# Three first loads on one DMA queue, and a longer run of zero matmuls

## The chip, the cores and the metric

The kernel runs on one core of a Trainium2 chip. A core has TensorE (PE in the profile: matmuls, with PEld for its weight loads), VectorE (DVE), ScalarE (ACT), GpSimd (POOL) and SyncE (SP), which issues DMAs. ACT can issue DMAs too, on a queue of its own; 16 DMA engines serve all queues. The metric is the time of one execution on the device in microseconds (us).

## The reference, cut to what matters

`x` has 2048 rows of 512 columns. One branch is attention with a window of 8 positions at a dilation of 2 and 32 heads of 16; the other is a token mixer over the 2048 rows with a layer norm and a GELU; a sigmoid gate mixes the two.

```python
g = sigmoid((x * gate_w).sum(-1, keepdims=True))
qkv = x @ wqkv                        # 512 x 1536: Wq, Wk, Wv side by side
logits[s, w] = (q[s] . k[s - 2*w]) * 16**-0.5      # w = 0..7, -1e9 before the start
a = (softmax(logits) weighted sum of v[s - 2*w]) @ wo
u = gelu(einsum("sd,sf->df", layernorm(x), w1) + b1)   # f = 1792
b = (u @ w2 + b2).T                   # back to 2048 x 512
out = g * a + (1 - g) * b
```

All tensors are bfloat16. Of the reference only the first product, `x @ wqkv`, matters here, and of it only the part that runs first: rows 0 to 511 of `x` against Wq and Wk.

## The kernel before

**Tiling.** TensorE contracts over the partitions, so it needs x transposed: `XT[p, d, s]` holds column 128·d + p of row s. The 512 columns of x make four slices d = 0..3, the 2048 rows four blocks `sb` of 512. Wq's rows come in the same four slices; the kernel calls each a quarter (128 KB, `ld_w(0, d, 1)` at L447; the first argument 0 is Wq, 1 is Wk, 2 is Wv, the last the number of slices). A group of matmuls for one slice d takes four, one for each output bank.

**Two ways to the transpose.** For block 0, slices 1 to 3 of XT come by a transposing DMA (`ld_xt0`, L470 to L476, issued at L473). Slice 0 comes otherwise: the plain columns 0 to 127 of rows 0 to 511 are loaded as they are into XP (`d_xp`, L479), TensorE transposes them with four matmuls against the identity matrix (`f_tr`, L544: tr0 and tr1), and ACT (L553, `ev_tra`) and VectorE (L555, `ev_trb`) each copy one half of the result into XT. The later blocks of XT come by transposing DMAs of 512 KB (`ld_xt`, L460).

**The zero matmuls.** Before and after the transposes TensorE runs matmuls on constants, whose results nobody reads (`f_warm`, L536, into bank 7): five of 512 columns and one of 256 ahead of the transposes (warm1, warm2), one of 512 behind them (warm3). The change's title calls these columns zeros; the operands are the constant 1.0, and the text keeps the title's word.

**The first projections.** The loop at L633 runs block 0's matmuls (L617): four for Wq with slice 0 (group 1), four each with slices 1, 2 and 3 (groups 2 to 4), then 16 for Wk in two halves. Group 1 waits for the two copies and Wq's first quarter, group 2 for the transposing DMA and Wq's second quarter, and so on; TensorE runs its work in order. ACT copies the finished banks to SBUF (L625 for block 0, L628 after). Then block 1 (32 matmuls), blocks 2 and 3, and Wv follow. Later TensorE works on the attention logits (L696), the mixer's two products (L810, L860) and the output projection (L876); VectorE ends with the sums of L897.

**What sets the order.** `_Sched` collects operations with their reads, writes and an estimated duration, and a list scheduler (L145) sorts each engine's work by estimated start times. For the first loads the estimates of landing are written in by hand (`lands`, L485 to L488), and `chain` (L941) fixes VectorE's and ACT's order for much of the kernel. A DMA belongs to the engine that issues it: `sch.dma("sp", ...)` or `sch.dma("act", ...)`. `after=prev_dma()` keeps SP's first loads in the order in which they are written, and later ones also wait until an earlier load has landed (`throttle`, L433). All direct DMAs are issued from L429.

Before the change SP issues, in this order: the transposing DMA of block 0, Wq's other three quarters, Wk in two halves, rows 0 to 255 of x for the layer norm (L439), the transposing DMA of block 1, and then the rest. ACT issues the plain columns and then Wq's first quarter.

Of the kernel before, what the change touches and what calls it, by code (L numbers as in the profile page):

```python
# [333 lines left out]
def bass_gated_mix__sliding_local_dilated__mixer_token_mlp__prompt_kernel(nc, A_x, A_wqkv, A_wo, B_x, B_w1, B_b1, B_w2, B_b2, gate_w, out, dbg=None):  # L334
    with contextlib.ExitStack() as es:
# [3 lines left out]
        sch = _Sched()  # L339

        x2d = A_x[0]
        xv = x2d.rearrange("(t p) d -> p t d", p=128)
# [72 lines left out]
        A = sch.add  # L415
# [12 lines left out]
        def mk_dma(dst, src):  # L428
            return lambda e: e.dma_start(dst, src)  # L429
# [3 lines left out]
        def throttle():  # L433
            return [init_dmas[-5]] if len(init_dmas) >= 5 else []

        def prev_dma():
            return [init_dmas[-1]] if init_dmas else []

        def ld_x(t0, n, q="sp"):  # L439
            ds = sch.dsem("x%d" % t0)  # L440
            op = sch.dma(q, mk_dma(X[:, t0:t0 + n, :], xv[:, t0:t0 + n, :]), n * 128 * D * 2, ds,
                         writes=["x%d" % t for t in range(t0, t0 + n)], deps=throttle() if q == "sp" else [], after=prev_dma() if q == "sp" else [], name="d_x%d" % t0)
            if q == "sp":
                init_dmas.append(op)
            return op

        def ld_w(tn, d0, n, q="sp"):  # L447
            ds = sch.dsem("wqkv%d_%d" % (tn, d0))
            op = sch.dma(q, mk_dma(WQKV[:, d0:d0 + n, tn * D:(tn + 1) * D], wqkv_v[:, d0:d0 + n, tn * D:(tn + 1) * D]),
                         n * 128 * D * 2, ds, writes=["wqkv%d_%d" % (tn, dt) for dt in range(d0, d0 + n)],  # L450
                         deps=throttle() if q == "sp" and n == 4 else [], after=prev_dma() if q == "sp" else [],
                         issue=0.65 if n == 4 else 0.45, name="d_wp%d_%d" % (tn, d0))
            if q == "sp":
                init_dmas.append(op)
            return op
# [14 lines left out]
        def ld_xt0():  # L470
            ds = sch.dsem("xt0")
            dst = XT[:, 1:4, 0:512]
            op = sch.dma("sp", lambda e: e.dma_start_transpose(dst, x2d[0:512, 128:512]), 512 * 384 * 2, ds, issue=1.25,  # L473
                         writes=XT0[1:4], after=prev_dma(), name="d_xt0")
            init_dmas.append(op)
            return op  # L476

        XP = view("OUTS", BF16, [(128, 4), (1, 128)])
        d_xp = sch.dma("act", mk_dma(XP, xv[:, 0:4, 0:128]), 512 * 128 * 2, sch.dsem("xp"), writes=["outs0"], issue=0.4, name="d_xp")  # L479

        first_loads = [ld_w(0, 0, 1, "act"), ld_xt0(), ld_w(0, 1, 1), ld_w(0, 2, 1), ld_w(0, 3, 1), ld_w(1, 0, 2), ld_w(1, 2, 2),
                       ld_x(0, 2)]
        ld_xt(1)
        first_loads.append(init_dmas[-1])
        for op_, t_ in zip(first_loads, (3.4, 4.6, 5.0, 5.4, 5.8, 6.6, 7.4, 8.2, 10.6)):  # L485
            op_.lands = t_
            op_.deps.clear()
        d_xp.lands = 3.1  # L488
# [11 lines left out]
        def ld_w1(j):  # L500
# [4 lines left out]
            if j < 4:  # L505
# [8 lines left out]
                       writes=["wo"], deps=throttle(), after=prev_dma(), name="d_wo")  # L514
# [4 lines left out]
        for i_, (v_, n_) in enumerate(((B_b1, NFT), (B_b2, NST))):  # L519
            vr = v_.rearrange("(t q j) -> q t j", q=4, j=32)  # L520
            for q_ in range(4):
                sch.dma("sp", mk_dma(psub(BR, 32 * q_, n_, 32 * i_, [(1, 32)]), vr[q_]), n_ * 64, ds_b, reads=["br"],
                        writes=["br_%d_%d" % (i_, q_)], deps=throttle(), after=prev_dma(), name="d_b_%d_%d" % (i_, q_), issue=0.45)
        d_w1.append(ld_w1(3))
        A("dve", lambda e: e.transpose(out=BT, in_=BR), 0.2, reads=["br_%d_%d" % (i_, q_) for i_ in range(2) for q_ in range(4)],
          writes=["btc"], name="t_b")
# [5 lines left out]
        def f_warm(n, w_=D):  # L532
            def fn(e):
                ins = None
                for _ in range(n):
                    ins = e.matmul(ps[:, 7, 0:w_], lhsT=CONE[:, 0:128], rhs=CONE[:, 0:w_], start=True, stop=True)  # L536
                return ins
            return fn

        def f_tr(h):  # L540
            def fn(e):
                ins = None
                for t in range(2):
                    ins = e.matmul(ps[:, 5 + h, 128 * t:128 * t + 128], lhsT=XP[:, 2 * h + t, :], rhs=IDENT, start=True, stop=True)  # L544
                return ins
            return fn
# [2 lines left out]
        w2_ = A("pe", f_warm(1, 256), 0.2, writes=["lg7_0", "lg7_1"], name="warm2", prio=-100)  # L549
        ta_ = A("pe", f_tr(0), 0.215, reads=["outs0", "ident"], writes=["lg5_0", "lg5_1"], after=[w2_], name="tr0", prio=-100)  # L550
        tr_ = A("pe", f_tr(1), 0.215, reads=["outs0", "ident"], writes=["lg6_0", "lg6_1"], after=[ta_], name="tr1", prio=-100)
        w3_ = A("pe", f_warm(1), 0.43, writes=["lg7_0", "lg7_1"], after=[tr_], name="warm3", prio=-100)
        A("act", lambda e: e.activation(out=XT[:, 0, 0:256], in_=ps[:, 5, 0:256], func=AF.Copy), 0.35, reads=["lg5_0", "lg5_1"],  # L553
          writes=["xt0_0"], name="ev_tra", prio=0)
        A("dve", lambda e: e.tensor_copy(out=XT[:, 0, 256:512], in_=ps[:, 6, 0:256]), 0.35, reads=["lg6_0", "lg6_1"],  # L555
          writes=["xt0_0b"], name="ev_trb", prio=0)
# [76 lines left out]
        for (b0, d0, d1, s0, s1) in ((0, 0, 1, 0, 512), (0, 1, 2, 0, 512), (0, 2, 3, 0, 512), (0, 3, 4, 0, 512), (4, 0, 2, 0, 512), (4, 2, 4, 0, 512)):  # L633
            for b in range(b0, b0 + 4):
# [3 lines left out]
                                 writes=fbn[b], after=[last_main[0]], name="pf_%s%d_%d_%d" % (tnames[tn], dl, d0, s0))  # L638
                last_main[0].order.add(w3_)
        for b, (tn, dl) in enumerate(first):  # L640
            A("act", f_evq(tn, dl, 0, b), 0.52, reads=fbn[b] + (["k5pad"] if tn == 1 else []),
              writes=["%s5_%d_0" % (tnames[tn], dl)], name="ev_%s%d_0" % (tnames[tn], dl), prio=0)
# [7 lines left out]
        for (tn, dl, sb) in seq_proj:  # L650
# [4 lines left out]
                             writes=["acc%d" % bank], after=[last_main[0]], name="pj_%s%d_%d" % (tnames[tn], dl, sb), prio=0)  # L655
            A("act", f_evq(tn, dl, sb, bank), 0.62, reads=["acc%d" % bank] + (["k5pad"] if tn == 1 else ["v5pad"] if tn == 2 else []),
              writes=["%s5_%d_%d" % (tnames[tn], dl, sb)], name="ev_%s%d_%d" % (tnames[tn], dl, sb), prio=0)
# [11 lines left out]
                writes=["xa"] + ["wqkv%d_%d" % (tn, dt) for tn in range(3) for dt in range(4)], name="d_xa")  # L669
        for t in range(NST):  # L670
# [5 lines left out]
          writes=["th"], name="g_tanh", prio=0)  # L676
# [31 lines left out]
        for wh in range(2):  # L708
# [6 lines left out]
            for (dl, c0, nc_) in pieces:  # L715
# [5 lines left out]
                  writes=wr, name="qkm_%d_%d_%d" % (wh, dl, c0), prio=0)  # L721
            rd = sum([pbn(b_) for b_ in bufs], []) + PBX[wh] + ["rp"]
            for wl in range(4):
                qop = A("pe", f_qkr(list(enumerate(bufs)), (wl,)), 0.92, reads=rd, writes=["lg%d_0" % (4 + wl), "lg%d_1" % (4 + wl)],
                        name="qkr_%d_%d" % (wh, wl), prio=-100 + wl, delay=BURST_DELAY)
                A("act", (lambda wh_, wl_: (lambda e: e.activation(out=ATT[:, :, 4 * wh_ + wl_, :], in_=ps[:, 4 + wl_, :].rearrange("p (h c) -> p h c", h=2), func=AF.Copy)))(wh, wl),  # L726
                  0.55, reads=["lg%d_0" % (4 + wl), "lg%d_1" % (4 + wl)], writes=["lw%d" % (4 * wh + wl)],
                  name="lev_%d_%d" % (wh, wl), prio=0)
# [60 lines left out]
        for k_, u in enumerate(USEQ):  # L789
# [7 lines left out]
            for (nm, n_, du) in (("ava", 4, 2.25), ("avb", 2, 1.2)):  # L797
                A("dve", (lambda pv_, n__: (lambda e: e.tensor_tensor(out=pv_[:, 0:n__], in0=pv_[:, 0:n__], in1=pv_[:, n__:2 * n__], op=ALU.add)))(pv, n_),  # L798
                  du, writes=[pn], name="%s_%d" % (nm, u))
# [27 lines left out]
        for ft in range(NFT):  # L827
# [6 lines left out]
              name="gel_%d" % ft, prio=0)  # L834
# [84 lines left out]
        for i in range(NST):  # L919
# [4 lines left out]
            elif i > 1:  # L924
# [6 lines left out]
              name="t1_%d" % i, prio=0)  # L931
# [119 lines left out]
```

## Time and profile before

| | |
|---|---|
| time, median of three runs | 168.57 us (168.3 to 168.81) |
| time of the profiled execution | 168.55 us |
| its span, first to last instruction | 167.3 us |
| TensorE / VectorE / ACT busy | 162.1 / 151.3 / 75.1 us |
| moved by DMA | 29.64 MB, 177 GB/s on average |
| first matmul of the projections | 5.61 us after the span's start |

All moments in the text are counted from the span's start. In a line of the timeline the columns are the start in us, the duration in us, the engine (a q behind it marks the engine's sequencer, which issues DMAs), the source line, the operation, what it writes and reads, and how many instructions were merged; a bracket gives the idle time of the engine before it and what ended that time. A duration of an issue is the time that the issuing engine spends, not the transfer; the landing is when the last of 16 arrivals is signalled. In a line of the DMA view q1 is SP's queue and q10 ACT's; the numbers are packets, MB, and the time that the packets took as a share of the 16 engines' time in the stretch (packets of one engine can overlap, so it can pass 100%).

### The profile page before, as it was taken

Reading aid. Unit: us, or ns where it says so; the run is one execution under the profiler, and the core shown is the slowest. Engines: PE = TensorE matmul, PEld = TensorE weight load, DVE = VectorE, ACT = ScalarE, POOL = GpSimd, SP = SyncE. Lnnn points to the kernel's source line nnn. Section 1 sums busy time; section 2 is a strip of 40 time slices with the busy share of each in tenths; the row PEclk is TensorE's granted clock in tenths of the full one; section 3 lists DMA queues with packets and bytes.
Section 4 is the critical chain, followed back from the end, with each engine's and each line's share of the span. In section 5 each row is a group of like instructions: output and inputs, shape, how many; then the busy total and the mean of one; then the engine's idle time right before and its main releaser. Section 6 shows DMA issues by size and latency. Waiting matters only on the chain.

```text
span 167.3 us, 2136 instructions
## 1 busy us (share of the span) xinstructions
PE 162.1 (97%) x845; PEld 77.5 (46%) x859; DVE 151.3 (90%) x154; ACT 75.1 (45%) x116; POOL 0.7 (0%) x8
## 2 busy tenths in 40 slices
PE   7699999999999999999999999999999999999994
PEld 2355555554454444444444444444444444444463
DVE  1055999999999999999999999999999999999896
ACT  3077688889899818793131121131231321310100
POOL 1000000000000000000000000000000000000000
PEclk9999999999999999999999999999999999999999
DMA  5999999959003846996779926462672570000454
GB/s 135 327 268 216 314 316 290 303 165 308 2 0 97 311 116 179 307 290 155 181 189 340 339 76 142 113 187 71 181 218 83 138 223 0 0 0 0 157 190 159
DMA packets 47625, 29.64 MB, mean 177 GB/s; under 512 B 9856, under 2 KB 46464, under 8 KB 47616
## 3 DMA queue, kind: packets, MB, share of 16 engines
q1 hardware_dynamic: 45120, 24.85, 54.4%
q10 hardware_dynamic: 2496, 4.66, 10.2%
q8 instruction: 7, 0.11, 0.3%
q14 instruction: 2, 0.02, 0.0%
HBM read 21.24 MB, written 2.10 MB: 140 GB/s over the span
## 4 chain that ended last, share of the span: by engine, by line
PE 91%; DMA 3%; DVE 2%; ACT 2%; issue 1%; ACTq 0%
PE ps L860 29%; PE ps L810 29%; PE ps L617 23%; PE ps L876 6%; PE ps L696 4%; DMA arena<-in_A_wqkv_dram 3%; DVE arena L897 2%; ACT L585 1%; ACT arena L628 1%; ACTq L429 0%; ACT arena L585 0%
## 5 line engine op out<-in xcount | busy, mean ns | idle before, releaser
L860 PE MATMUL ps<-arena 128*128 128x512 bf16 x220 | 48.5, 379 | 0.2
L810 PE MATMUL ps<-arena 128*128 128x512 bf16 x219 | 48.2, 379 | 0.4 <-issue 0.2
L617 PE MATMUL ps<-arena 128*128 128x512 bf16 x188 | 41.4, 379 | 1.6 <-DMA arena<-in_A_wqkv_dram 1.3
L688 DVE TENSOR_TENSOR arena<-arena 128x4096 bf16<-128x4096 bf16 (+1 forms) x12 | 35.5, 2998 | 2.5 <-ACT arena L628 2.1
L795 DVE TENSOR_TENSOR arena<-arena 128x8192 bf16<-128x8192 bf16 x8 | 35.0, 4419 | 0.0
L860 PEld LDWEIGHTS ps<-arena 128*128 128x128 bf16 x224 | 21.9, 98 | 26.4
L810 PEld LDWEIGHTS ps<-arena 128*128 128x128 bf16 x224 | 21.8, 98 | 26.6 <-ACT arena L726 0.4
L617 PEld LDWEIGHTS ps<-arena 128*128 128x128 bf16 x192 | 21.6, 113 | 21.5 <-issue 1.8
L928 ACT ACTIVATE arena<-ps,arena 128x512 bf16<-128x512 f32 x16 | 12.5, 778 | 39.4 <-PE ps L860 39.4
L798 DVE TENSOR_TENSOR arena<-arena 128x4096 bf16<-128x4096 bf16 (+1 forms) x16 | 27.0, 1751 | 0.0
L628 ACT ACTIVATE arena<-ps 128x512 bf16<-128x512 f32 x32 | 18.6, 596 | 4.5 <-PE ps L617 4.5
L831 ACT ACTIVATE arena<-ps,arena 128x512 bf16<-128x512 f32 x14 | 9.6, 687 | 22.2 <-PE ps L810 16.6
L572 DVE BATCH_NORM_STATS2 arena<-arena 128x6 f32<-128x512 bf16 x16 | 10.0, 682 | 6.1 <-DMA arena<-in_A_x_dram 6.1
L876 PE MATMUL ps<-arena 128*128 128x512 bf16 (+1 forms) x79 | 14.1, 336 | 0.1
L897 DVE SCALAR_TENSOR_TENSOR arena<-ps,arena 128x512 bf16<-128x512 f32 (+1 forms) x20 | 11.5, 637 | 0.9 <-PE ps L876 0.7
L596 ACT ACTIVATE arena<-arena 128x512 bf16<-128x512 bf16 x16 | 12.2, 804 | 0.0
L625 ACT ACTIVATE arena<-ps 128x512 bf16<-128x512 f32 x16 | 9.0, 597 | 6.2 <-PE ps L617 6.1
L876 PEld LDWEIGHTS ps<-arena 128*128 128x128 bf16 x80 | 7.8, 98 | 6.2
L672 DVE SCALAR_TENSOR_TENSOR arena<-arena 128x512 bf16<-128x512 bf16 x16 | 10.1, 689 | 0.0
L742 DVE TENSOR_TENSOR arena<-arena 128x512 bf16<-128x512 bf16 (+4 forms) x11 | 7.3, 667 | 0.6 <-ACT arena L761 0.2
L696 PE MATMUL ps<-arena 128*32 128x512 bf16 x128 | 7.3, 380 | 0.0
L726 ACT ACTIVATE arena<-ps 128x512 bf16<-128x512 f32 x8 | 4.7, 592 | 4.6 <-PE ps L696 4.6
(42 smaller groups left out, 40.0 us busy)
## 6 DMA issues: line engine op xcount, KB each, us to landing
arena<-in_B_w_dram SPq DMA_DIRECT2D x7, 1024.0 KB, 8.5
arena<-in_B_w_dram SPq DMA_DIRECT2D x8, 896.0 KB, 5.2
arena<-arena ACTq DMA_DIRECT2D x32, 128.0 KB, 2.9
arena<-in_A_x_dram SPq DMA_DIRECT2D x4, 512.0 KB, 6.1
out_dram<-arena SPq DMA_DIRECT2D x14, 128.0 KB, 1.7
arena<-in_A_x_dram SPq DMA_DIRECT2D x1, 1536.0 KB, 7.9
arena<-in_A_wqkv_dram SPq DMA_DIRECT2D x2, 256.0 KB, 3.8
arena<-in_A_x_dram SPq DMA_DIRECT2D x2, 256.0 KB, 3.6
```

The costliest lines, as they stand in the source:

```text
L596: A("act", (lambda t_: (lambda e: e.activation(out=X[:, t_, :], in_=X[:, t_, :], func=AF.Identity, scale=col(RSTD, t_), bias=col(NMR, t_)) ...
L617: ins = e.matmul(ps[:, bank, s0:s1], lhsT=lhsT, rhs=XT[:, dt, sb * 512 + s0:sb * 512 + s1], start=(dt == 0 and s0 == 0), stop=(dt == 3))
L628: return lambda e: e.activation(out=dst, in_=ps[:, bank, :], func=AF.Copy)
L688: return lambda e: e.tensor_tensor(out=PBL[buf][:, :, 512 * c0:512 * (c0 + nc_)], in0=in0, in1=in1, op=ALU.mult)
L696: ins = e.matmul(ps[32 * c:32 * c + 32, 4 + wl, :], lhsT=RP, rhs=PBL[buf][:, wl, c * 512:(c + 1) * 512], start=(dl == 0), stop=(dl == 3), ...
L795: A("dve", (lambda o_, i0, i1: (lambda e: e.tensor_tensor(out=o_, in0=i0, in1=i1, op=ALU.mult)))(pv, in0, in1), 4.4, reads=v_res + ["atx_% ...
L798: A("dve", (lambda pv_, n__: (lambda e: e.tensor_tensor(out=pv_[:, 0:n__], in0=pv_[:, 0:n__], in1=pv_[:, n__:2 * n__], op=ALU.add)))(pv, n ...
L810: ins = e.matmul(ps[:, bank, :], lhsT=W1W[:, slot, st, 128 * e_:128 * e_ + 128], rhs=X[:, st, :], start=(st == 0), stop=(st == NST - 1))
L860: ins = e.matmul(ps[:, bank, :], lhsT=W2S[slot][:, ft, 128 * e_:128 * e_ + 128], rhs=UT[:, ft, :], start=(ft == 0), stop=(ft == NFT - 1))
L876: ins = e.matmul(ps[:, bank, 0:c1 - c0], lhsT=OT[:, t, 128 * i:128 * i + 128], rhs=WO[:, t, c0:c1], start=(t == 0), stop=(t == 3))
L897: A("dve", (lambda i_, b_, c0_, c1_: (lambda e: e.scalar_tensor_tensor(out=T1[:, i_, c0_:c1_], in0=ps[:, b_, 0:c1_ - c0_], scalar=col(G, i ...
L928: A("act", (lambda i_, bank_: (lambda e: e.activation(out=T1[:, i_, :], in_=ps[:, bank_, :], func=AF.Identity, scale=col(OMG, i_), bias=co ...
```

## The change

The plain columns and Wq's first quarter are issued by SP instead of ACT, ahead of the transposing DMA. SP's order becomes: plain columns, Wq's first quarter, transposing DMA of block 0, Wq's other quarters, and the rest as before. ACT issues no DMA at the start. The planner's landing estimates are written anew (that of block 1's transposing DMA stays). Behind the transposes TensorE runs one more constant matmul of 256 columns, which becomes the one after which the projections are ordered.

```diff
-        d_xp = sch.dma("act", mk_dma(XP, xv[:, 0:4, 0:128]), 512 * 128 * 2, sch.dsem("xp"), writes=["outs0"], issue=0.4, name="d_xp")
+        d_xp = sch.dma("sp", mk_dma(XP, xv[:, 0:4, 0:128]), 512 * 128 * 2, sch.dsem("xp"), writes=["outs0"], issue=0.4, name="d_xp")

-        first_loads = [ld_w(0, 0, 1, "act"), ld_xt0(), ld_w(0, 1, 1), ld_w(0, 2, 1), ld_w(0, 3, 1), ld_w(1, 0, 2), ld_w(1, 2, 2),
+        first_loads = [ld_w(0, 0, 1), ld_xt0(), ld_w(0, 1, 1), ld_w(0, 2, 1), ld_w(0, 3, 1), ld_w(1, 0, 2), ld_w(1, 2, 2),
                        ld_x(0, 2)]
...
-        for op_, t_ in zip(first_loads, (3.4, 4.6, 5.0, 5.4, 5.8, 6.6, 7.4, 8.2, 10.6)):
+        for op_, t_ in zip(first_loads, (3.5, 4.9, 5.3, 5.7, 6.1, 6.9, 7.7, 8.5, 10.6)):
...
-        w3_ = A("pe", f_warm(1), 0.43, writes=["lg7_0", "lg7_1"], after=[tr_], name="warm3", prio=-100)
+        A("pe", f_warm(1), 0.43, writes=["lg7_0", "lg7_1"], after=[tr_], name="warm3", prio=-100)
+        w3_ = A("pe", f_warm(1, 256), 0.2, writes=["lg7_0", "lg7_1"], after=[tr_], name="warm4", prio=-100)
```

## The prediction

> **What bounds the kernel now.** I read the share of each engine first, then the chain that ended last in order of time, then the waits of TensorE, then the start second by second, because the first three leave only the start open.
>
> ```profile
> PE 162.1 (97%) x845; PEld 77.5 (46%) x859; DVE 151.3 (90%) x154; ACT 75.1 (45%) x116; POOL 0.7 (0%) x8
> ```
>
> ```profile
> 0.80 0.46 ACTq L429
> 1.25 0.03 issue
> 1.28 4.24 DMA arena<-in_A_wqkv_dram
> 5.52 0.09 issue
> 5.61 8.36 PE ps L617 x38
> ...
> 161.67 3.98 DVE arena L897 x9
> ```
>
> ```profile
> PE ps L617 <- DMA arena<-in_A_wqkv_dram: 1.3, 1, 1.3
> PE ps L536 <- PEq L1036: 0.8, 1, 0.8
> PE ps L617 <- ACT arena L585: 0.2, 1, 0.2
> PE ps L810 <- issue: 0.2, 1, 0.2
> ```
>
> TensorE is busy for 97% of the span. The chain (its first and last pieces) shows why: up to 5.52 us it is one load, Wq's first quarter issued by ACT at 1.28; from 5.61 it is almost all TensorE, up to 161.64, where VectorE's last sums begin. TensorE's only wait of weight is the one for that quarter; the two of 0.2 are the size of one matmul, and some records are missing. So 161.64 - 5.61 = 156.0 us run without a hole, and the end moves one for one with the start of this stream, as long as its later operands are there in time. The span is 167.3, the profiled execution took 168.55, so 1.25 lies outside the span; the three runs have a median of 168.57. I sum against 168.55. About 0.3% (0.5 us) is what a measurement of this kernel can tell from no change, and my bounds for faster and slower are that.
>
> The start, in the timelines of SP, ACT, TensorE and VectorE:
>
> ```profile
> 0.80 1.35 SPq L473 DMA_TRANSPOSE arena<-in_A_x_dram  x1
> 2.22 2.49 SPq L429 DMA_DIRECT2D arena<-in_A_wqkv_dram  x5
> 0.80 0.46 ACTq L429 DMA_DIRECT2D arena<-in_A_x_dram  x1
> 1.28 0.53 ACTq L429 DMA_DIRECT2D arena<-in_A_wqkv_dram  x1
> 1.84 1.28 ACT L553 ACT_TABLE_LOAD   x1 [1.84 <-issue]
> 3.74 0.38 ACT L553 ACTIVATE arena<-ps 128x256 bf16<-128x256 f32 x1 [0.62 <-PE ps L544]
> 3.96 0.42 DVE L555 CAST arena<-ps 128x256 bf16<-128x256 f32 x1 [2.45 <-PE ps L544]
> 0.84 2.51 PE L536 MATMUL ps<-const-bfloat16-1.0 128*128 128x512 bf16 x6 [0.84 <-PEq L1036]
> 3.33 0.58 PE L544 MATMUL ps<-arena 128*128 128x128 bf16 x4
> 3.71 0.63 PE L536 MATMUL ps<-const-bfloat16-1.0 128*128 128x512 bf16 x1
> 5.61 3.62 PE L617 MATMUL ps<-arena 128*128 128x512 bf16 x16 [1.26 <-DMA arena<-in_A_wqkv_dram]
> ```
>
> SP issues the transposing DMA at once, ACT the plain columns (xp) and Wq's first quarter. The trace has the landings: xp 3.20, Wq's first quarter 5.52, transposing DMA 5.74, Wq's second quarter (SP, issued 2.22) 5.98, third 6.22, fourth 6.59. The stream's matmuls start 0.216 us apart: group 1 (four, Wq's first quarter) from 5.61, group 2 (four, needs the transposing DMA and Wq's second quarter) from 6.47. So group 2 could already start at 5.98 + 0.09 = 6.07; the slack behind the first wait is only 0.40. This is the key reading: it is not enough to bring Wq's first quarter forward, the transposing DMA and the second quarter must come no later than 6.47 - 0.09 = 6.38.
>
> **The change, part by part.**
>
> *Plain columns on SP instead of ACT.* Issued at 0.80 on either queue. They land at 3.20, or up to 0.2 earlier if no other transfer runs beside them (from about 2.5 the transposing one did). The zeros in front end at 2.93 + 0.21 = 3.14, so the transposes start at 3.14 to 3.33 and VectorE's copy (3.96 + 0.42 = 4.38) ends at 4.2 to 4.38. Nothing gained by itself: Wq's quarter is later.
>
> *Wq's first quarter on SP, second.* Issued at 1.28 again (0.80 + 0.46 and a gap of 0.03). What it loses is the company of the transposing DMA. The DMA view of two stretches (2.0 to 2.5, then 2.9 to 3.4; packets, MB, share) shows that company:
>
> ```profile
> q10 hardware_dynamic: 299, 0.08, 66.6%
> ```
>
> ```profile
> q1 hardware_dynamic: 556, 0.14, 126.9%
> ```
>
> ACT's queue (q10) alone moves in the first, SP's (q1) alone in the second, while ACT's Wq quarter has been issued since 1.28; its first packet runs at 3.46. Bounds for its landing: 3.6 (xp's 3.20 plus 128 packets of 1,024 bytes at 46 ns over 16 engines, 0.37) and the old 5.52. At both, group 1 starts between 4.45 (after VectorE's copy) and 5.61 and ends by 6.47 at the latest. So group 1 leaves the path; late next are the transposing DMA and Wq's second quarter.
>
> *The transposing DMA third on SP.* Its issue moves from 0.80 to 0.80 + 0.46 + 0.53 + two gaps of 0.03 = 1.85, a slip of 1.05, and every later DMA of SP slips with it: Wq's second quarter from 2.22 to 3.27, then two more quarters, two loads of Wk, x and the second transposing DMA, in that order on the one queue. How much of the slip reaches the landings is the unknown. Upper bound: all 1.05. Lower bound: none, since the DMA engines, busy without a break from 2.0 on, and not SP set the pace, and four of the 16 engines, which bring the last arrivals of the second quarter at 5.98 where twelve have theirs by 5.51, may not lag when one queue feeds them; that would even gain 0.47. In between stands a sum from packets. xp and Wq's quarter are through at about 2.08 + 0.5 + 0.37 = 2.95. The transposing DMA's first packet came 1.74 after its issue began (2.54 for 0.80), so now at 3.59: the engines stand empty for 0.64. Its 1,536 packets at 556 in 0.5 us take 1.38, to 4.97, and the second quarter's 128 take 0.4 (as before, 4.94 to 5.33 for the third), to 5.37. Before, that last packet ended at 4.94: a slip of 0.43. I take 0.5, nearest to this sum, for a rate that two queues together raised (shares above 100%). Then the second quarter lands at 5.98 + 0.5 = 6.48, the transposing DMA at 6.24, and group 2 starts at 6.57 instead of 6.47: +0.10. The third and fourth quarters land near 6.7 and 7.1, needed at 7.43 and 8.30.
>
> [...]
>
> *Further down SP's queue.* Even the whole 1.05 is covered: the second transposing DMA lands at 10.73 and is needed after 32 matmuls, at 12.52 (cover 1.8); the fourth at 18.31 against 20.29; VectorE's statistics on x end at 13.0 and its next work waits to 15.07 for ACT. If a cover were gone, each 0.1 would cost 0.1.
>
> *No load on ACT.* Its table load (1.84, 1.28 long) may start up to 1.05 earlier; its next work waits for the transposes until 3.74. Worth nothing.
>
> *256 more columns of zeros.* Cold matmuls of 512 start 0.427 apart, so 0.21, from 4.14 to 4.35: inside the idle stretch, before VectorE's copy ends. If the copy is done at 4.2, it delays group 1 by 0.15, which the wait of group 2 hides.
>
> Sum: 0 for xp, group 1, ACT and the zeros, +0.10 at group 2: 168.55 + 0.10 = 168.65, told as 168.7.
>
> **Rivals.**
>
> *No lag, so faster.* If all 16 engines keep step, the second quarter lands at 5.51 + 0.43 = 5.94 and group 2 starts at 6.03: -0.44, 168.1; the earliest I can build is 5.9 (-0.57, 168.0). For: the lag shows where two queues overlap. Against: late arrivals on a few engines stand also in loads at 19.7 to 21.3, when SP alone issues.
>
> *SP's issue sets the landing, so slower.* If the queue is served a fixed time after each issue, the second quarter lands at 5.98 + 1.05 = 7.03 and group 2 starts at 7.12: +0.65, 169.2. It decides from a landing after 6.38. For: Wq's first quarter needed 2.18 from issue to first packet, and by that figure the second quarter's would come at 5.45, near the sum's end. [...]
>
> *The clock.* Zeros and transposes keep TensorE busy from 0.84 to 4.14, at 0.427 per 512 columns; group 1 runs at 0.216. In the new order TensorE pauses again between groups 1 and 2, near 5.3 to 6.5. If half speed lasted into the stream, each matmul would cost 0.21 more: 8 of them 1.7, 170.3. Against: a pause of 1.47 (4.14 to 5.61) did no harm before. [...]
>
> *The planner's order.* Its stream starts 0.3 later against unchanged due times (4.06 to 4.22, then 5.06 to 5.36), so neighbours may change places. TensorE's other waits are 0.2 each: plus or minus 0.4.
>
> **How the numbers follow.** Likeliest case 0.46 (same 0.42, slower 0.04), no lag 0.20 (faster 0.15, same 0.05), SP's issue 0.24 (slower 0.23, same 0.01), clock 0.05 (slower), order 0.05 (faster 0.02, slower 0.03). Together faster 0.17, same 0.48, slower 0.35. The likeliest case's own range is 168.4 to 169.0; to hold 8 in 10 it must take in both ends of the slip, 168.1 to 169.3.
>
> **What would show it.** Wq's first quarter lands before 4.6 and TensorE's first wait for it shrinks under 0.5; a new wait of about 1.2 stands between matmuls four and five, ended by Wq's second quarter or the transposing DMA; group 2 starts at 6.5 to 6.6; no other wait of TensorE grows. I am wrong if group 2 starts outside 6.0 to 7.2, if the matmuls after it are more than 0.216 apart, or if a wait opens after 12 us.

## The result, and the profile after

The changed kernel takes 169.06 us (median of 11 runs, 168.69 to 169.39) beside 168.35 for the kernel before (11 runs, 167.72 to 170.62): a ratio of 1.0048, 95% interval 1.0026 to 1.0069, so slower by the prediction's bound of 0.5 us. The ratio is taken over fast runs, without the one of 170.62. The predicted 168.7 was 0.36 too low; the range of 168.1 to 169.3 holds the time. The likeliest case (same) did not come about; slower had 0.35.

To understand the numbers one has to know that single runs of the kernel before fall into two groups: over the four comparisons of this study 76 of 104 lie from 167.57 to 168.90 (mean 168.10) and 28 from 169.85 to 170.81 (one run of 614.63 us is left out). The changed kernel has one group, all its 23 runs from 168.58 to 169.39. So its median is 0.8 above the earlier median of 168.27, its mean (169.04) only 0.35 above the earlier mean (168.69), and the profiled run of before (168.55) was a late one of the lower group.

The profiled run of the changed kernel took 168.69, its fastest. Its share of engines and the first and last pieces of its chain:

```profile
PE 163.2 (97%) x846; PEld 77.5 (46%) x860; DVE 151.3 (90%) x154; ACT 75.0 (45%) x116; POOL 0.7 (0%) x8
```

```profile
0.80 0.45 SPq L429
1.25 0.06 issue
1.31 0.49 SPq L429
1.80 0.05 issue
1.85 1.64 SPq L473
3.48 0.05 issue
3.54 2.81 DMA arena<-in_A_wqkv_dram
6.34 0.14 issue
6.48 7.43 PE ps L618 x33
...
161.82 3.98 DVE arena L898 x9
```

The chain now begins with three issues of SP in a row and then with Wq's second quarter (issued 3.54, landed 6.34) instead of the first. TensorE's stream goes on from 6.48, where it stood at 6.47 before at the same matmul, and VectorE's last sums begin at 161.82 instead of 161.67. The timelines of SP and TensorE, then TensorE's one wait of the stream for a load (source lines are one higher than before, behind the added one):

```profile
1.85 1.64 SPq L473 DMA_TRANSPOSE arena<-in_A_x_dram  x1
3.54 2.51 SPq L429 DMA_DIRECT2D arena<-in_A_wqkv_dram  x5
6.09 0.47 SPq L429 DMA_DIRECT2D arena<-in_A_x_dram  x1
6.60 3.85 SPq L460 DMA_TRANSPOSE arena<-in_A_x_dram  x1
10.49 1.09 SPq L429 DMA_DIRECT2D arena<-in_A_x_dram  x2
```

```profile
3.19 0.58 PE L544 MATMUL ps<-arena 128*128 128x128 bf16 x4
3.57 0.84 PE L536 MATMUL ps<-const-bfloat16-1.0 128*128 128x512 bf16 x2
4.29 1.90 PE L618 MATMUL ps<-arena 128*128 128x512 bf16 x4
6.48 7.87 PE L618 MATMUL ps<-arena 128*128 128x512 bf16 x34 [0.29 <-DMA arena<-in_A_wqkv_dram]
```

```profile
PE ps L618 <- DMA arena<-in_A_wqkv_dram: 0.3, 1, 0.3
```

The four matmuls from 4.29 are group 1; that they take 1.90 says that they ran at half speed, 0.427 apart. The wait behind them is ended by Wq's second quarter. One thing is new that no wait of TensorE above names: in the timeline of its weight loads there is a pause at block 1.

```profile
12.10 0.11 PEld L618 LDWEIGHTS ps<-arena 128*128 128x128 bf16 x1
12.64 0.36 PEld L618 LDWEIGHTS ps<-arena 128*128 128x128 bf16 x3 [0.43 <-ACT arena L629]
```

The view puts it down to ACT, but ACT's copy of that bank was the one of 8.62, done at 9.22. What came 0.10 before is the landing of the second transposing DMA, 12.54 (10.73 before). In the trace the matmul due at 12.53 starts at 12.67, a hole of 0.145; with 0.01 from group 2 that is the whole difference of the two spans (167.43 and 167.28). Landings of the two profiled runs:

| load | before: issue, landing | changed: issue, landing | slip of the landing | needed in the changed stream |
|---|---|---|---|---|
| Wq's first quarter | 1.28, 5.52 | 1.31, 3.95 | -1.57 | |
| transposing DMA, block 0 | 0.80, 5.74 | 1.85, 5.75 | 0.01 | group 2 |
| Wq's second quarter | 2.22, 5.98 | 3.54, 6.34 | 0.36 | group 2 |
| Wk's first half | 3.77, 7.46 | 5.10, 9.00 | 1.54 | 9.07 |
| transposing DMA, block 1 | 5.27, 10.73 | 6.60, 12.54 | 1.81 | 12.53 |
| transposing DMA, block 3 | 13.62, 18.31 | 15.62, 20.09 | 1.78 | 20.4 |

The slip grows along SP's queue: 0.36 where the prediction worked it out, 1.5 to 1.8 where it only bounded it. For SP's later issues, the same rows of its timeline before the change:

```profile
5.27 3.36 SPq L460 DMA_TRANSPOSE arena<-in_A_x_dram  x1
8.67 1.09 SPq L429 DMA_DIRECT2D arena<-in_A_x_dram  x2
```

Two landings now fall on the very moment at which they are needed. But this run lost only 0.15; why most runs lose 0.4 more is the question of the experiments. Engines, DVE and ACT included, run the same work in the same order in both kernels apart from the edit itself, so a changed plan is out.

### The profile page after: what moved, and what is told of

Read it like the earlier page. It is cut to its first block, busy times and chain, and to the rows that moved or that the text cites. A ratio compares the mean times of both kernels' runs of the same rounds, so it can differ in the third digit from the quotient of the medians.

```text
span 167.4 us, 2138 instructions
## 1 busy us (share of the span) xinstructions
PE 163.2 (97%) x846; PEld 77.5 (46%) x860; DVE 151.3 (90%) x154; ACT 75.0 (45%) x116; POOL 0.7 (0%) x8
## 4 chain that ended last, share of the span: by engine, by line
PE 92%; DVE 2%; DMA 2%; SPq 2%; issue 1%
PE ps L861 29%; PE ps L811 29%; PE ps L618 24%; PE ps L877 6%; PE ps L697 4%; DVE arena L898 2%; DMA arena<-in_A_wqkv_dram 2%; SPq L473 1%; SPq L429 1%
```

## The experiments

Each experiment was to tell apart some of five theories. C: the covers are gone, and later loads stop the stream in most runs. K: TensorE's clock, by which the author means matmuls at half speed, 0.427 apart instead of 0.216, that last into the stream; the profile's PEclk reads 1.00 at both spacings (4.29 to 5.98 and 6.48 to 8.00 in the changed kernel), so a clock as the cause is the author's reading. L: late arrivals of the first loads. W: Wq's second quarter. S: the serial issue on SP itself.

**The changed kernel again.** No edit.

> The changed kernel once more, for another execution and for the comparison with the next three. Theory C (covers): the longer issue on SP makes the second transposing DMA and Wk's first half land just when the stream needs them (12.54 against a need at 12.53 in the first profile), so executions differ by holes of 0.1 to 0.7 us near 9.1 and 12.5 us; this profile then shows such a hole again and the time is 168.7 to 169.4. Theory K (clock): in the slower executions TensorE is still at half speed (0.427 us apart) in group 2, and the profile shows that in some execution; time the same. Theory L (lag): the changed kernel loses nothing new, but the kernel before has executions whose first loads land without four late arrivals, near 167.8, and the changed one cannot start so early; then the stream starts group 2 at 6.4 to 6.6 with no hole and the time beside before is +0.3 to +0.9.

Measured: 169.08 (12 runs, 168.58 to 169.22), beside before 1.0035 (1.0009 to 1.0062). Its profiled run starts group 2 at 6.37 and has a hole elsewhere, 0.134 where the matmuls for Wk begin. The weight loads show it, and here the view names the load itself (landed 9.10):

```profile
8.59 0.11 PEld L618 LDWEIGHTS ps<-arena 128*128 128x128 bf16 x1
9.14 0.36 PEld L618 LDWEIGHTS ps<-arena 128*128 128x128 bf16 x3 [0.45 <-DMA arena<-in_A_wqkv_dram]
```

The second transposing DMA came at 12.47 this time and stopped nothing. So C's holes are there, one or the other, as expected; their size in a typical run is still open.

**The order without the zeros.**

```diff
-        A("pe", f_warm(1), 0.43, ..., name="warm3", prio=-100)
-        w3_ = A("pe", f_warm(1, 256), 0.2, ..., name="warm4", prio=-100)
+        w3_ = A("pe", f_warm(1), 0.43, ..., name="warm3", prio=-100)
```

> The changed order of the loads without the 256 further columns. Theory C and theory L: the zeros do nothing, so 169.0, within 0.25 of the run before it. Theory K: a shorter busy stretch brings full speed later, so slower by 0.2 to 0.9, up to 170.

Measured: 169.27 (12 runs, 168.78 to 169.71), 0.2 above the changed kernel, at the edge of both expectations. What counts more: none of its runs is in an upper group. It is the order, not the 256 columns, that removes it.

**The zeros alone.** The kernel before with the same 256 columns.

> The kernel before with the 256 further columns alone. Theories C and L: as the kernel before, 168.35 within 0.25, since the columns lie in the wait for Wq's first quarter. Theory K: the longer busy stretch helps or does nothing; 167.8 to 168.4.

Measured: 168.50 (12 runs), but in two groups as before: seven from 167.64 to 168.74 and five from 170.02 to 170.87. The columns by themselves change nothing that can be seen. Neither expectation had the two groups in it; the lower one is where both put the time.

**The second transposing DMA one place earlier.** The planner's landing estimates are changed to fit.

```diff
 first_loads = [..., ld_w(1, 0, 2), ld_w(1, 2, 2),
-                       ld_x(0, 2)]
+                       ]
         ld_xt(1)
         first_loads.append(init_dmas[-1])
+        first_loads.append(ld_x(0, 2))
```

> The changed kernel with the second transposing DMA issued before the first rows of x for the layer norm, so that it lands some 0.8 us earlier (near 11.7) and x later. Theory C: the hole near 12.5 closes; 0.15 to 0.5 faster than the changed kernel, 168.5 to 168.7. Theories K and L: no change, 169.0 within 0.2, and the profile shows no hole near 12.5 but the same start of group 2.

Measured: 168.83 (12 runs, 168.39 to 169.64), on the same chip as the repeated kernel at 169.08: 0.25 faster. In its profile the DMA lands at 11.65 and the hole near 12.5 is gone, although group 2 starts late in that run, at 6.87. The gain lies in C's 0.15 to 0.5; the time itself is 0.13 above C's 168.5 to 168.7.

**TensorE kept busy in the old order.** The kernel before with three further matmuls of 512 columns.

```diff
-        w3_ = A("pe", f_warm(1), 0.43, ..., name="warm3", prio=-100)
+        A("pe", f_warm(1), 0.43, ..., name="warm3", prio=-100)
+        w3_ = A("pe", f_warm(3), 0.2, ..., name="warm4", prio=-100)
```

> The order of before, with three further zero matmuls of 512 columns that keep TensorE busy from 4.14 to about 5.4 at half speed, the stretch in which it waits for Wq's first quarter. The times of the kernel before fall into two groups, 167.7 to 168.9 and 169.9 to 170.7. Theory K (clock): the upper group are executions in which the pause from 4.14 on left TensorE at half speed into the stream; with the pause filled the upper group vanishes and all times lie in 167.7 to 169.2, spread by the moment at which full speed comes. Theory L (late arrivals of the first loads make the groups): the upper group stays at a third of the executions, near 170.

Measured: 168.57 (12 runs, 167.94 to 169.01), none in the upper group, where the kernel before had 4 of 25 beside it. With 28 of 104 over all, 12 runs without one would come by chance about once in 43; with the 4 of 25 beside it, once in 8. So this speaks for K against L, and does not settle it alone. The ratio is 1.0023 (1.0004 to 1.0042): it buys a narrow spread and no better median.

**Few zeros.** One matmul of 512 columns in front instead of five.

```diff
-        A("pe", f_warm(5), 2.13, writes=["lg7_0", "lg7_1"], name="warm1", prio=-100)
+        A("pe", f_warm(1), 2.13, writes=["lg7_0", "lg7_1"], name="warm1", prio=-100)
```

> The order of before with one zero matmul of 512 columns in front instead of five, so TensorE is busy only 0.84 to 1.5 and 3.2 to 4.1 before the stream. Theory K: every execution starts the stream at half speed, 0.427 us apart, for 1.5 to 4 us: 169.8 to 171 always, and the profile shows the first 8 to 16 matmuls at 0.427. Theory L: two groups as before.

Measured: 168.90, 169.62, 170.21 and 171.38. A wider spread than expected, but the profiled run (169.62) shows a half-speed start:

```profile
0.83 0.80 PE L536 MATMUL ps<-const-bfloat16-1.0 128*128 128x512 bf16 x2 [0.83 <-PEq L1036]
3.27 0.58 PE L544 MATMUL ps<-arena 128*128 128x128 bf16 x4 [1.65 <-DMA arena<-in_A_x_dram]
3.65 0.63 PE L536 MATMUL ps<-const-bfloat16-1.0 128*128 128x512 bf16 x1
4.60 5.63 PE L617 MATMUL ps<-arena 128*128 128x512 bf16 x16 [0.31 <-DMA arena<-in_A_wqkv_dram]
```

Sixteen matmuls take 5.63 where the profile of before has 3.62 for them: 0.427 apart up to 8.4, then 0.216. The same lines show a second thing: the order is that of before, and yet the stream starts at 4.60, a whole 1.0 earlier, because Wq's first quarter landed at 4.51 and not at 5.52. Here its 16 arrivals came within 0.2; in the profile of before the last four came 0.9 to 1.0 after the twelfth. So both kinds of start occur in the old order, and with full speed the early kind would give times near 167.6 (168.55 less 0.9).

**Wq's first quarter alone on SP.** Plain columns on ACT, no further zeros.

```diff
-        first_loads = [ld_w(0, 0, 1, "act"), ld_xt0(), ...
+        first_loads = [ld_w(0, 0, 1), ld_xt0(), ...
-        first_loads[0].order.add(d_xp)
```

> One part alone: Wq's first quarter on SP ahead of the transposing DMA, the plain columns stay on ACT, no further zeros. SP slips by half as much. Theory S (the serial issue on SP delays the transposing DMA and all behind it, by 0.9 at the issue of Wq's second quarter in the changed kernel's profile: 3.54 for 2.22 less a shorter way): the second quarter lands at about 6.1, group 2 starts at 6.1 to 6.2, between the two kernels: 168.4 to 168.7. Theory K: group 1 starts near 4.4, so no pause before it and no upper group near 170. Theory L: the upper group stays.

Measured: 169.13 (12 runs, 168.15 to 170.40), a miss: I expected 168.4 to 168.7 and no run near 170. The profiled run, the fastest, is as S had it (second quarter 5.86, group 2 at 6.00). But the plain columns land at 3.67, so TensorE pauses for 0.46 between the first zeros and the transposes, and four of the runs lie from 169.8 up.

**Wq's second quarter on ACT.**

```diff
-        first_loads = [ld_w(0, 0, 1), ld_xt0(), ld_w(0, 1, 1), ld_w(0, 2, 1), ...
+        first_loads = [ld_w(0, 0, 1), ld_xt0(), ld_w(0, 1, 1, "act"), ld_w(0, 2, 1), ...
```

> The changed kernel with Wq's second quarter issued by ACT at once, so that only the transposing DMA and not that quarter stands behind SP's serial issue. Theory S: group 2 then waits for the transposing DMA alone (5.65 to 5.75, or up to 0.4 later for the quarter's packets in between) and starts at 5.8 to 6.2; the loads behind it come one issue (0.6) earlier: 168.2 to 168.8, faster than the changed kernel by 0.3 to 0.8. Theory K alone, in which the changed kernel's typical times above its profile come from full speed arriving late: 168.8 to 169.2 in most executions, since the clock does not arrive earlier.

Measured: 169.12 (9 runs, 168.87 to 170.22), no gain. The profile says where it went in that run. Group 2 starts at 6.23, 0.25 earlier than in the changed kernel, and even follows group 1 without a wait (the plain columns landed late, at 3.82 for 3.05, and held group 1 back to 5.05). The second transposing DMA, whose issue takes 4.21 here, lands at 12.72:

```profile
5.05 7.38 PE L618 MATMUL ps<-arena 128*128 128x512 bf16 x32
12.86 1.25 PE L618 MATMUL ps<-arena 128*128 128x512 bf16 x5 [0.42 <-ACT arena L629]
```

The hole is 0.58 and takes back more than the gain: in this run the faster start is worth nothing, because the next load in SP's queue is already the bound. The times alone do not single out this cause, since K had 168.8 to 169.2 for most runs, and seven of the nine lie there.

**No need for the second transposing DMA.** Block 1's projections for Wq and Wk read block 0.

```diff
-            xr = xt_of(sb)
+            xb = 0 if sb == 1 and tn < 2 else sb
+            xr = xt_of(xb)
...
-            last_main[0] = A("pe", f_proj(tn, dl, sb, bank), 0.866,
+            last_main[0] = A("pe", f_proj(tn, dl, xb, bank), 0.866,
```

> The changed kernel, but block 1's projections onto Wq and Wk read block 0 of the transpose, so that TensorE never waits for the second transposing DMA, which is still issued (this part of the output is wrong). Theory C (covers gone): executions of the changed kernel lie up to 0.7 above its profile because this landing (12.25 to 12.54 in the profiles, needed from 12.4 to 12.6) is often later; without the need the median falls from 169.07 by 0.25 or more, to 168.6 to 168.8. Theory W (Wq's second quarter): the median stays at 169.0 to 169.1, since the time is set by the start of group 2.

Measured: 168.93 (10 runs, 168.56 to 169.32): 0.14 below the changed kernel's 169.07, less than C wanted, and on another chip. In its profile the DMA lands at 12.94, 0.4 after the usual need, and the stream does not stop there; it stops for Wk's first half (landed 9.12, a hole of 0.18).

**No need for Wk's halves either.** In addition, the first matmuls for Wk read Wq's weights.

```diff
-                 f_proj(tn, dl, 0, b, d0, d1, s0, s1)
+                 f_proj(0, dl, 0, b, d0, d1, s0, s1)
-                 reads=xt_of(0, d0, d1) + ["wqkv%d_%d" % (tn, dt) for dt in range(d0, d1)],
+                 reads=xt_of(0, d0, d1) + ["wqkv0_%d" % dt for dt in range(d0, d1)],
```

> As the run before it, and the first matmuls for Wk read Wq's weights, so that the start waits for no load behind Wq's fourth quarter (both parts of the output are wrong). Theory C: 168.4 to 168.7, down by 0.4 or more from 169.07, what Wk's first half (9.0 to 9.1, needed at 9.0 to 9.1) takes in addition. Theory W: 169.0 to 169.1 still.

Measured: 168.64 (12 runs, 168.44 to 169.21), 0.29 below the run before it on the same chip and 0.43 below the changed kernel (medians of 169.06 and 169.08; the second is from another chip, the chip of the first is not on record; the kernel before is no faster on this one, 168.32 beside 168.25). C's number; W, which said 169.0 to 169.1, falls. What is left, 168.64, is next to the prediction's sum of 168.65, but that is chance: in the profile group 2 starts at 6.37, not at 6.57, and the run loses time further down. The profiled run is the slowest of the twelve, and shows that the list of late loads does not end at block 1:

```profile
4.41 15.99 PE L618 MATMUL ps<-arena 128*128 128x512 bf16 x67
20.87 1.46 PE L618 MATMUL ps<-arena 128*128 128x512 bf16 x6 [0.47 <-DMA arena<-in_A_x_dram]
```

Block 3's transposing DMA lands at 20.74, and TensorE stands still for 0.64.

**Only the first quarter and the transposing DMA needed.** In addition, all of block 0's matmuls read Wq's first quarter.

```diff
-            lhsT = sub(WQKV, dt * 3 * D + tn * D + dl, [(4, 128)])
+            lhsT = sub(WQKV, (0 if w0 else dt) * 3 * D + tn * D + dl, [(4, 128)])
...
-                 f_proj(0, dl, 0, b, d0, d1, s0, s1)
+                 f_proj(0, dl, 0, b, d0, d1, s0, s1, w0=True)
-                 reads=xt_of(0, d0, d1) + ["wqkv0_%d" % dt for dt in range(d0, d1)],
+                 reads=xt_of(0, d0, d1) + ["wqkv0_0"],
```

> As the run before it, and all of block 0's matmuls read Wq's first quarter, so that the stream waits for that quarter and the transposing DMA alone. Theory W: the second quarter is late in most executions (last arrivals up to 1.0 after the others), so this falls by 0.5 or more against the run before it, to 168.0 to 168.2. Theory C: by what group 2 gains in the profiles, 5.65 to 5.75 for the landing of the transposing DMA against 6.24 to 6.34, so 0.55 to 0.65, from 168.5 to 167.9. Both give a gain; the run before it tells them apart, and this one tells how much the second quarter's place behind the transposing DMA costs. If full speed comes late in most executions (theory K), it gains less than 0.3.

Measured: 168.46 (12 runs, 167.88 to 169.32), a gain of 0.18 where W and C wanted 0.5 or more; under 0.3 is what K had said. In the profiled run (167.99) group 2 starts at 5.57, 0.8 earlier than in the run before, and part of that is given back at block 3, whose transposing DMA lands at 19.61 and leaves a hole of 0.34. Full speed came at 3.9 in that run, ahead of the stream. In a run in which it comes at 6.4, as in the profile of the run before, an earlier group 2 would, by the author's estimate from these two moments, run at half speed until then. Whether block 3 or half speed takes the missing 0.3 in the other runs was not tried.

**Wq's first quarter alone on SP, with zeros up to group 1.**

```diff
-        w2_ = A("pe", f_warm(1, 256), 0.2, ..., name="warm2", prio=-100)
+        w2_ = A("pe", f_warm(2, 448), 0.2, ..., name="warm2", prio=-100)
...
+        w3_ = A("pe", f_warm(1, 256), 0.2, ..., name="warm4", prio=-100)
```

> Wq's first quarter on SP ahead of the transposing DMA, the plain columns on ACT, as in e7_wq_sp, and the zeros extended so that TensorE has no pause before group 1: two of 448 columns ahead of the transposes instead of one of 256, and 256 further ones behind them. Theory K: the executions of e7_wq_sp at 169.7 to 170.4 are half-speed starts; they vanish, and the times gather at 168.1 to 168.9. Theories C and W: the spread stays, 168.2 to 170.4.

Measured: 168.79 (12 runs, 168.37 to 169.45), no run above, where the same order without the zeros had four of twelve from 169.8 up. As K expected, though three of the runs lie above its 168.9. It is between the two kernels, 1.0032 (1.0002 to 1.0061) of before.

No version tried has a better median than the kernel before.

## Why the prediction was right or wrong

**The start sets the end, one for one: right.** From the start of group 2 to TensorE's last end the trace has 158.65 us in the profile of before, and 158.65 in those of the order alone, the zeros alone and the DMA moved up, which have no hole behind group 2. In that of the changed kernel it is 158.80, longer by its hole.

**Group 1 leaves the path: right.** Wq's first quarter lands at 3.95 (predicted 3.6 to 5.52), group 1 starts at 4.29, after VectorE's copy. It ran at half speed (0.427 apart) for 1.7 us, where the prediction had 0.216 per matmul; the wait for group 2 hides that.

**Group 2 by +0.10: right in the profile, and in good part by luck.** 6.48 against 6.57 predicted, with a slip of the second quarter's landing of 0.36 against 0.5. Two errors hide in it. The packets slipped more than the sum had it: the transposing DMA's issue grew (1.64 against 1.35), so SP slipped by 1.32, not 1.05; its packets ran from 3.23 to 5.19 and took 1.96, not 1.38, and the second quarter's last packet ended at 5.71, not 5.37 (before: 4.94). Against that the late arrivals of the no-lag rival mostly went away: the landing came 0.63 after the last packet instead of 1.04, and for the transposing DMA 0.55 instead of 1.20, so that it landed at 5.75 as before and not at 6.24. The 0.5 itself stood above the sum's 0.43 for a rate that two queues together raised, and the runs show no such rate: in the profile of before the engines moved 286 GB/s from 2.5 to 2.9, when both queues had packets, and 285 from 2.9 to 3.4, when SP's alone had.

**"Even the whole 1.05 is covered": wrong, and this is the step that failed.** It bounded the slip of later loads by the slip of their issue and so costed them at nothing. Measured, the second transposing DMA slipped by 1.81 against a cover of 1.8, Wk's first half, which the step did not even list, by 1.54 against a cover of 1.6 (7.46 for a need at 9.06). In the median these two together cost 0.43 (169.07 to 168.64; drawing the runs anew at random, an estimate, gives 0.2 to 0.6). How they share it is not shown: taking away the first need gave 0.14 and the second 0.29, both within the scatter of the runs, while moving the second transposing DMA up gave 0.25 by itself. The term that should have stood there as +0.4 stood at 0. One of the prediction's own signs of being wrong, a wait that opens after 12 us, is the hole of 0.145 in the profile. Why the slip grows is shown only in part: SP issues are 1.3 later from the second quarter on, the second transposing DMA's own issue takes 3.85 instead of 3.36, and what SP issues behind it is 1.8 later. The engines also moved less: from 3 to 6 us 219 GB/s (209 in the repeated kernel), where the profile of before has 312. Why they moved less was not tried. Why the landing of Wk's half slips by 0.2 more than its issue stays open (its last arrivals come 1.1 after the twelfth, before 0.24).

**Base: half wrong.** I took the profiled run for the kernel. It had the four late arrivals, which I made the condition of the rival that makes the changed kernel faster; but the kernel before has early starts too (4.60 in one profile of its order), so its lower group reaches down to 167.57, and the change was measured against that. Of the 0.8 between the medians, 168.64 less 168.27, or 0.37, is left when none of these late loads is needed; it belongs to the base and to the start.

**The rivals.** SP's issue setting the landing did not happen at group 2, where I had placed it (Wq's second quarter issued 1.32 later, landed 0.36 later), but it happened further down (the second transposing DMA 1.33 and 1.81). The clock, feared for the new pause, works the other way round: the new order starts group 1 at 4.29 instead of 5.61, fills TensorE's pause of 1.47 (4.14 to 5.61) and removes the upper group. That the upper group are half-speed starts was not seen in a profile of such a run; it is argued from the experiments that fill the pause (none in 12, none in 12) against those that do not (5 of 12; and, in the order with late plain columns, 4 of 12 from 169.8 up), and from the run with few zeros, whose profile does show such a start. The planner's order did not change at all.

## What to carry to other kernels

When a DMA is put in front of others on one queue, list every load behind it with its landing and its need, and let the slip grow along the queue: here 1.05 at the issue of the third became 1.8 at the landing of the tenth, and two covers of 1.6 and 1.8 were used up. One profile of a start-up is one draw: look at the spread of the runs first, and do not take the arrivals of one execution for the kernel's. Filling a pause of TensorE before the main stream narrowed the spread here (167.94 to 169.01), and gained nothing in the mean: 168.53 with it, and 168.47 in the 25 runs of the kernel before beside it.

## What the runs showed of the hardware

The moment at which TensorE passes from 0.427 to 0.216 us per 512 columns, read from the matmul starts, differs from run to run with nearly the same work in front of it: 3.7 in the profiles with the zeros alone and without the need for the second transposing DMA, 3.9 with the first quarter only, 4.5 with zeros up to group 1, 4.9 with that DMA moved up, 5.7 with the second quarter on ACT, 6.4 in the repeated kernel, 6.8 with the old order's pause filled; 8.7 with few zeros. TensorE starts at 0.83 or 0.84 in all. Without the last value these moments spread over 3.1. The 8.7 comes where TensorE had paused for 1.65 us, and the passage at 3.7 came 2.9 us after TensorE's first matmul. What sets the moment was not shown.

The issue of a transposing DMA is not a fixed cost: the one of block 1 held SP for 3.36 in the profile of before and 3.19 to 4.87 is the range for those of blocks 1 and 2 in all profiles, and nothing behind it on the queue is issued meanwhile (in the profile of before it ends at 8.63 and the next issue starts at 8.67). The issues of the two loads that moved to SP are short beside their transfers: 0.45 and 0.49 in the profile of the changed kernel, landings 2.25 and 2.64 after their start. They add up all the same: with their gaps they put the transposing DMA's issue back by 1.05 (1.85 for 0.80), and the tenth load of the new order was issued 1.33 later and landed 1.81 later.
